# Decode attention with grouped queries: 8 MB loads through two buffers, a TensorE loop over the heads, and both projections moved out of it

## The chip, the cores and the metric

The kernel runs on one core of one Trainium2 chip. The core has five engines that run side by side, each in the order of its own instructions: TensorE (PE, with its weight loads listed as PEld), VectorE (DVE), ScalarE (ACT), GpSimd (POOL) and SyncE (SP). Data comes from HBM through 16 DMA engines, which take transfers from queues; here nearly all transfers are issued by SP, on one queue. The metric is the time on the device in microseconds, the median of several runs. Lower is better.

## The reference

One decode step of a transformer block, in float32, for one token `x` of 512 numbers:

```python
h  = x + A(layernorm(x))      # A: attention over a cache
h2 = h + B(layernorm(h))      # B: bilinear GLU

def A(x):                     # 32 query heads, 8 key/value heads, 65,536 cached positions, 128 wide
    q = x @ wq                                    # 512 -> 32 x 128
    scores = q . k / sqrt(128)                    # each group of 4 query heads shares one k and v
    o = softmax(scores) . v                       # over all 65,536 positions
    return o.reshape(4096) @ wo                   # 4096 -> 512

def B(x):
    return ((x @ w_gate) * (x @ w_up)) @ w_down   # 512 -> 1792 -> 512
```

K and V are 268 MB each, the five weight matrices together 28 MB. Every byte of them is used once.

## The kernel before, in words

K is laid out transposed in HBM. Each of the 8 heads (a key/value head with its four query heads) goes through K in eight tiles of 4 MB (128 partitions with 8,192 numbers each, 32 KB a row), then through V in eight tiles of 4 MB. All these tiles, and the large weights at the end, pass through one pool `stream` of four buffers (line 45), each loaded by one DMA from SP (`load`, line 107). A load waits until PE has finished with the buffer's last tile.

The order of the instructions on each engine, and the waits between engines, come from a tile framework: the code is written in sequence, the framework adds the semaphores, and every instruction of every head is its own (nothing loops on the chip).

A head runs like this. wq's share for this head (1 MB) is loaded into the pool `wts`; 16 small matmuls with the weights as the stationary side give the four query vectors as columns (line 139), and DVE puts them into a zero-padded `q_pad` (line 142). For a K tile, 16 matmuls with 512 columns write scores into one PSUM bank (line 154); the padding places each result in its own row, so that two tiles fill a bank of 128 rows. ACT copies a full bank to SBUF (line 160), DVE takes row maxima (line 161). After the last K tile the maxima are joined by a transpose on PE, a reduction, and a matmul that spreads them over the partitions (lines 165 to 177). ACT takes the exponential with row sums (line 184), PE transposes the probabilities (line 188), DVE copies them out (line 191). Then `pva` is zeroed by matmuls with a tile of zeros (line 218), and V's tiles are multiplied into it (line 232). DVE copies the rows out, four matmuls fold them to columns (line 242), and the result is divided by the sum. wo's share of this head (1 MB) is multiplied at once and added to `attn`, which gathers over the heads (line 249).

After the last head come the sum with x (folded into `attn` by matmuls on `x_oct`, line 212), the second layernorm, gate and up projection (line 285), the product, and the down projection into `pd` (line 323). wg is one load; wu comes in three pieces and wd in five, of falling size (lines 253 to 261). The output is stored at line 328.

Of the kernel before, what the change touches and what calls it, by code (L numbers as in the profile page):

```python
# [1 line left out]

# [6 lines left out]
F32 = mybir.dt.float32  # L18
AF = mybir.ActivationFunctionType
ALU = mybir.AluOpType  # L20
# [6 lines left out]
CK = 8192  # L27
# [5 lines left out]
NC = F // P  # L33
SCALE = DH ** -0.5
EPS = 1e-5


@with_exitstack
def body(ctx: ExitStack, tc: tile.TileContext, xc, xr, kT, v, wq, wo, wg, wu, wd, out):
    nc = tc.nc  # L40
    PS = bass.MemoryType.PSUM
    const = ctx.enter_context(tc.tile_pool(name="const", bufs=1))
    stream = ctx.enter_context(tc.tile_pool(name="stream", bufs=4))
    wts = ctx.enter_context(tc.tile_pool(name="wts", bufs=2))
    sbig = ctx.enter_context(tc.tile_pool(name="sbig", bufs=6))
    small = ctx.enter_context(tc.tile_pool(name="small", bufs=2))
    ps_sc = ctx.enter_context(tc.tile_pool(name="ps_sc", bufs=2, space=PS))
    ps_tp = ctx.enter_context(tc.tile_pool(name="ps_tp", bufs=2, space=PS))
    ps_va = ctx.enter_context(tc.tile_pool(name="ps_va", bufs=1, space=PS))
    ps_at = ctx.enter_context(tc.tile_pool(name="ps_at", bufs=1, space=PS))  # L50
    ps_sm = ctx.enter_context(tc.tile_pool(name="ps_sm", bufs=2, space=PS))

    def ctile(shape, name):
        return const.tile(shape, F32, tag=name, name=name)

    x_col = ctile([P, KT], "x_col")
    nc.scalar.dma_start(x_col, xc)
    ident = ctile([P, P], "ident")
    make_identity(nc, ident)
    mean_m = ctile([P, P], "mean_m")  # L60
    nc.vector.memset(mean_m, 1.0 / D)
    ones = ctile([P, P], "ones")
    nc.vector.memset(ones, 1.0)
    eps_t = ctile([P, 1], "eps_t")
    nc.vector.memset(eps_t, EPS)
    sel_h = ctile([P, REP], "sel_h")
    nc.vector.tensor_reduce(
        out=sel_h, in_=ident.rearrange("p (g h) -> p h g", h=REP), axis=AX.X, op=ALU.add)
    x_oct = ctile([8, D // 8], "x_oct")
    sel_b = ctile([P, 16], "sel_b")  # L70
    nc.vector.tensor_reduce(
        out=sel_b, in_=ident.rearrange("p (j c) -> p c j", j=4)[:, 0:16, :], axis=AX.X, op=ALU.add)
    sel_q = ctile([P, 4], "sel_q")
    nc.vector.tensor_copy(sel_q, ident.rearrange("p (j c) -> p c j", j=4)[:, 0, :])
    sel_1 = ctile([P, 1], "sel_1")
    nc.vector.tensor_reduce(out=sel_1, in_=sel_q, axis=AX.X, op=ALU.add)
    neg_mean = ctile([P, P], "neg_mean")
    nc.vector.tensor_scalar(
        out=neg_mean, in0=mean_m, scalar1=sel_1[:, 0:1], scalar2=-1.0, op0=ALU.mult, op1=ALU.mult)

    PADW = 2 * 28 + REP
    q_pad = [ctile([P, PADW], f"q_pad{i}") for i in range(2)]
    o_pad = [ctile([P, REP, 32], f"o_pad{i}") for i in range(2)]
    hn_pad = ctile([P, KT, 32], "hn_pad")
    f_pad = ctile([P, NC, 32], "f_pad")
    sel_pad = ctile([P, 32], "sel_pad")
    zeros = ctile([P, 512], "zeros")
    for t in (*q_pad, *o_pad, hn_pad, f_pad, sel_pad, zeros):
        nc.gpsimd.memset(t, 0.0)

    nc.vector.tensor_copy(sel_pad[:, 0:1], sel_1)

    def rstd_of(c, name):

        sq = small.tile([P, KT], F32, tag="ln_q", name=f"{name}_q")
        nc.vector.tensor_tensor(out=sq, in0=c, in1=c, op=ALU.mult)
        s2 = small.tile([P, 1], F32, tag="ln_s", name=f"{name}_s2")
        nc.vector.tensor_reduce(out=s2, in_=sq, axis=AX.X, op=ALU.add)
        pv = ps_sm.tile([P, 512], F32, tag="sm", name=f"{name}_pv")
        nc.tensor.matmul(pv[:, 0:1], mean_m, s2, start=True, stop=True)  # L100
        std = small.tile([P, 1], F32, tag="ln_t", name=f"{name}_t")
        nc.scalar.activation(std, pv[:, 0:1], AF.Sqrt, bias=eps_t[:, 0:1], scale=1.0)
        rstd = small.tile([P, 1], F32, tag="ln_r", name=f"{name}_r")
        nc.vector.reciprocal(rstd, std)
        return rstd

    def load(shape_cols, src, name, parts=P):
        t = stream.tile([P, CK], F32, tag="stream", name=name)
        nc.sync.dma_start(t[:parts, :shape_cols], src)  # L109
        return t  # L110

    wq_sb = wts.tile([P, KT, 512], F32, tag="wq", name="wq0")
    nc.sync.dma_start(wq_sb, wq[0])  # L113

    xn = ctile([P, KT], "xn")
    s1 = small.tile([P, 1], F32, tag="ln_s", name="ln1_s")
    nc.vector.tensor_reduce(out=s1, in_=x_col, axis=AX.X, op=ALU.add)
    pm = ps_sm.tile([P, 512], F32, tag="sm", name="ln1_pm")
    nc.tensor.matmul(pm[:, 0:1], mean_m, s1, start=True, stop=True)
    mean = small.tile([P, 1], F32, tag="ln_m", name="ln1_m")  # L120
    nc.vector.tensor_copy(mean, pm[:, 0:1])
    xd = small.tile([P, KT], F32, tag="ln_d", name="ln1_d")
    nc.vector.tensor_scalar(
        out=xd, in0=x_col, scalar1=mean[:, 0:1], scalar2=None, op0=ALU.subtract)
    rstd1 = rstd_of(xd, "ln1")
    nc.vector.tensor_scalar(  # L126
        out=xn, in0=xd, scalar1=rstd1[:, 0:1], scalar2=None, op0=ALU.mult)

    attn = ps_at.tile([P, 512], F32, tag="attn", name="attn")

    for h in range(HKV):
        if h > 0:
            wq_sb = wts.tile([P, KT, 512], F32, tag="wq", name=f"wq{h}")
            nc.sync.dma_start(wq_sb, wq[h])
        pq = ps_sm.tile([P, 512], F32, tag="sm", name=f"pq{h}")
        for r in range(REP):
            for k in range(KT):
                nc.tensor.matmul(  # L138
                    pq[:, r:r + 1], wq_sb[:, k, r * P:(r + 1) * P], xn[:, k:k + 1],
                    start=(k == 0), stop=(k == KT - 1))  # L140
        qp = q_pad[h % 2]
        nc.vector.tensor_copy(qp[:, 28:28 + REP], pq[:, 0:REP])

        scores = []
        mx = small.tile([P, 4], F32, tag="mx", name=f"mx{h}")
        for s in range(NT // 2):
            psc = ps_sc.tile([P, 512], F32, tag="sc", name=f"psc{h}_{s}")
            for half in range(2):
                n = 2 * s + half
                kt = load(CK, kT[h, n], f"k{h}_{n}")  # L150
                for r4 in range(4):
                    rs = 4 * half + r4
                    for j in range(4):
                        nc.tensor.matmul(  # L154
                            psc[32 * j:32 * j + 32, :],
                            qp[:, 28 - 4 * rs:60 - 4 * rs],
                            kt[:, (4 * r4 + j) * 512:(4 * r4 + j + 1) * 512],
                            start=(rs == 0), stop=(rs == 7))
            sc = sbig.tile([P, 512], F32, tag="scores", name=f"sc{h}_{s}")
            nc.scalar.copy(sc, psc)  # L160
            nc.vector.tensor_reduce(out=mx[:, s:s + 1], in_=sc, axis=AX.X, op=ALU.max)  # L161
            scores.append(sc)

        m1 = small.tile([P, 1], F32, tag="m1", name=f"m1_{h}")
        nc.vector.tensor_reduce(out=m1, in_=mx, axis=AX.X, op=ALU.max)  # L165
        pmx = ps_sm.tile([P, 512], F32, tag="sm", name=f"pmx{h}")
        nc.tensor.transpose(pmx[0:1, 0:P], m1, ident)  # L167
        mrow = small.tile([1, REP], F32, tag="mrow", name=f"mrow{h}")
        nc.vector.tensor_reduce(
            out=mrow, in_=pmx[0:1, 0:P].rearrange("p (g h) -> p h g", h=REP), axis=AX.X, op=ALU.max)  # L170
        mexp = small.tile([1, 32, REP], F32, tag="mexp", name=f"mexp{h}")
        nc.vector.tensor_copy(mexp, mrow.unsqueeze(1).to_broadcast([1, 32, REP]))  # L172
        pmb = ps_sm.tile([P, 512], F32, tag="sm", name=f"pmb{h}")
        nc.tensor.matmul(  # L174
            pmb[:, 0:1], mexp.rearrange("p g h -> p (g h)"), ones[0:1, 0:1], start=True, stop=True)
        nbias = small.tile([P, 1], F32, tag="nbias", name=f"nbias{h}")
        nc.vector.tensor_scalar(  # L177
            out=nbias, in0=pmb[:, 0:1], scalar1=-SCALE, scalar2=None, op0=ALU.mult)

        sums = small.tile([P, 4], F32, tag="sums", name=f"sums{h}")  # L180
        probs = []
        for s in range(NT // 2):
            sc = scores[s]
# [184 lines left out]
```

## Time and profile before

| | |
|---|---|
| median of 3 runs | 1320.65 us (1320.31 to 1320.68) |
| profiled execution: span from first to last instruction | 1319.2 us |
| median less that span | 1.45 us |
| PE busy, PE instructions (matmuls and weight loads) | 62%, 9,876 |
| DVE, ACT busy | 5%, 4% |
| DMA: bytes read, mean rate | 564.66 MB, 429 GB/s |
| granted TensorE clock, mean | 0.754 |
| instruction fetches by DMA | 38 packets, 0.62 MB |

The page divides the span into 40 slices. The chain of waits is followed back from the last instruction: each piece is either work or a transfer that was being waited for. The windows list, for a stretch of time, the busy time of each engine, the granted clock, the mean busy share of the 16 DMA engines and the bytes per second. Of the profiled execution the profile gives the span alone; what lies around it is taken as the 1.45 us between the span and the median.

### The profile page before, as it was taken

Reading aid. Unit: us, or ns where it says so; the run is one execution under the profiler, and the core shown is the slowest. Engines: PE = TensorE matmul, PEld = TensorE weight load, DVE = VectorE, ACT = ScalarE, POOL = GpSimd, SP = SyncE. Lnnn points to the kernel's source line nnn. Section 1 sums busy time; section 2 is a strip of 40 time slices with the busy share of each in tenths; the row PEclk is TensorE's granted clock in tenths of the full one; section 3 lists DMA queues with packets and bytes.
Section 4 is the critical chain, followed back from the end, with each engine's and each line's share of the span. In section 5 each row is a group of like instructions: output and inputs, shape, how many; then the busy total and the mean of one; then the engine's idle time right before and its main releaser. Section 6 shows DMA issues by size and latency. Waiting matters only on the chain.

```text
span 1319.2 us, 10572 instructions
## 1 busy us (share of the span) xinstructions
PE 818.6 (62%) x4938; PEld 244.9 (19%) x4938; DVE 66.8 (5%) x170; ACT 47.9 (4%) x104; POOL 2.2 (0%) x14
## 2 busy tenths in 40 slices
PE   5566476665757566665665666556575555665567
PEld 3111031211212112121211212112121121211114
DVE  1000000100001000010000100001000010000000
ACT  0010000100001000010000100001000000001000
POOL 0000000000000000000000000000000000000000
PEclk9867877767776787776877768777777777877767
DMA  9999999999999999999999999999999999999997
GB/s 401 434 436 429 430 435 432 435 433 431 430 437 430 433 431 434 434 432 430 434 435 430 432 434 431 437 430 432 432 435 433 430 432 430 438 431 431 431 430 314
DMA packets 22674, 565.33 MB, mean 429 GB/s; under 512 B 2660, under 2 KB 2664, under 8 KB 3304
## 3 DMA queue, kind: packets, MB, share of 16 engines
q1 hardware_dynamic: 22488, 564.67, 99.4%
q8 instruction: 38, 0.62, 0.2%
q10 hardware_dynamic: 144, 0.00, 0.0%
q14 instruction: 4, 0.03, 0.0%
HBM read 564.66 MB, written 0.00 MB: 428 GB/s over the span
## 4 chain that ended last, share of the span: by engine, by line
DMA 85%; PE 14%; issue 0%; SPq 0%; DVE 0%
DMA k<-in_kT 42%; DMA v<-in_v 41%; PE psc L154 7%; PE pva L232 7%; DMA wd<-in_wd 2%; PE pd L323 0%; SPq L109 0%; SPq L113 0%; DVE y L327 0%
## 5 line engine op out<-in xcount | busy, mean ns | idle before, releaser
L154 PE MATMUL psc<-k,q_pad 128*32 128x512 f32 x2048 | 345.7, 837 | 227.4 <-DMA k<-in_kT 227.4
L232 PE MATMUL pva<-v,pt 128*16 128x512 f32 x2048 | 338.3, 821 | 216.9 <-DMA v<-in_v 216.9
L154 PEld LDWEIGHTS psc<-k,q_pad 128*32 128x32 f32 x2048 | 83.6, 147 | 492.7 <-issue 293.9
L232 PEld LDWEIGHTS pva<-v,pt 128*16 128x16 f32 x2048 | 66.4, 122 | 481.6 <-DMA v<-in_v 271.2
L160 ACT COPY sc<-psc 128x512 f32<-128x512 f32 x32 | 18.8, 586 | 1147.7 <-PE psc L154 1147.7
L161 DVE TENSOR_REDUCE mx<-sc 128x1 f32<-128x512 f32 x32 | 22.0, 686 | 584.3 <-ACT sc L160 584.3
L138 PE MATMUL pq<-xn,wq 128*128 128x1 f32 x256 | 39.3, 288 | 0.8 <-DVE xn L126 0.8
L138 PEld LDWEIGHTS pq<-xn,wq 128*128 128x128 f32 x256 | 38.8, 243 | 0.9 <-DVE xn L126 0.9
L188 PE MATMUL ptp<-ident,sc 128*128 128x128 f32 x128 | 30.5, 413 | 10.9 <-ACT sc L184 10.5
L239 DVE COPY orow<-pva 128x512 f32<-128x512 f32 x8 | 5.5, 692 | 553.4 <-PE pva L232 553.4
L218 PE MATMUL pva<-zeros 128*32 128x512 f32 x64 | 26.7, 1025 | 0.0
L249 PE MATMUL attn<-wo,o_pad 128*32 128x512 f32 x64 | 26.5, 1049 | 0.3 <-DVE o_pad L246 0.3
L188 PEld LDWEIGHTS ptp<-ident,sc 128*128 128x128 f32 x128 | 23.0, 212 | 15.9 <-ACT sc L184 12.2
L184 ACT ACTIVATE sc<-sc,nbias 128x512 f32<-128x512 f32 x32 | 22.7, 711 | 18.5 <-DVE nbias L177 18.5
L191 DVE COPY pt<-ptp 128x512 f32<-128x512 f32 x32 | 22.1, 692 | 23.0 <-PE ptp L188 22.3
L242 PE MATMUL po<-sel_b,orow 128*128 128x4 f32 x64 | 8.5, 256 | 6.5 <-DVE orow L239 6.5
L242 PEld LDWEIGHTS po<-sel_b,orow 128*128 128x128 f32 x64 | 7.8, 191 | 13.9 <-DVE orow L239 13.9
L167 PE MATMUL pmx<-ident,m 128*1 128x128 f32 x8 | 2.2, 270 | 12.4 <-DVE m L165 12.4
L202 PE MATMUL pl<-l,ones 128*128 128x4 f32 x16 | 4.3, 339 | 7.4 <-DVE l L199 7.4
L174 PE MATMUL pmb<-ones,mexp 1*128 1x1 f32 x16 | 3.8, 306 | 5.0 <-DVE mexp L172 5.0
L323 PE MATMUL pd<-wd,f_pad 128*32 128x128 f32 x112 | 6.1, 417 | 1.2 <-DMA wd<-in_wd 1.2
L323 PEld LDWEIGHTS pd<-wd,f_pad 128*32 128x32 f32 x112 | 5.8, 174 | 1.2 <-DVE f_pad L318 1.2
(76 smaller groups left out, 72.8 us busy)
## 6 DMA issues: line engine op xcount, KB each, us to landing
k<-in_kT SPq DMA_DIRECT2D x64, 4096.0 KB, 34.3
v<-in_v SPq DMA_DIRECT2D x63, 4096.0 KB, 35.0
wq<-in_wq SPq DMA_DIRECT2D x8, 1024.0 KB, 34.8
wo<-in_wo SPq DMA_DIRECT2D x8, 1024.0 KB, 35.4
v<-in_v SPq DMA_DIRECT2D x4, 1024.0 KB, 30.3
wg<-in_wg SPq DMA_DIRECT2D x1, 3584.0 KB, 31.7
wu<-in_wu SPq DMA_DIRECT2D x1, 1792.0 KB
wu<-in_wu SPq DMA_DIRECT2D x2, 896.0 KB, 27.3
```

The source lines that it names most:

```text
L138: nc.tensor.matmul(pq[:, r:r + 1], wq_sb[:, k, r * P:(r + 1) * P], xn[:, k:k + 1], start=(k == 0), stop=(k == KT - 1))
L154: nc.tensor.matmul(psc[32 * j:32 * j + 32, :], qp[:, 28 - 4 * rs:60 - 4 * rs], kt[:, (4 * r4 + j) * 512:(4 * r4 + j + 1) * 512], start=(rs ...
L160: nc.scalar.copy(sc, psc)
L161: nc.vector.tensor_reduce(out=mx[:, s:s + 1], in_=sc, axis=AX.X, op=ALU.max)
L184: nc.scalar.activation(sc, sc, AF.Exp, bias=nbias[:, 0:1], scale=SCALE, accum_out=sums[:, s:s + 1])
L188: nc.tensor.transpose(ptp[:, b * P:(b + 1) * P], sc[:, b * P:(b + 1) * P], ident)
L191: nc.vector.tensor_copy(pt.rearrange("p g b h -> p b g h"), ptp.rearrange("p (b g h) -> p b g h", b=4, h=REP))
L218: nc.tensor.matmul(pva[32 * j:32 * j + 32, :], zeros[:, 0:32], zeros, start=True, stop=False)
L232: nc.tensor.matmul(pva[32 * j:32 * j + 16, :], pt[:, 8 * j + rs, :, :].rearrange("p b h -> p (b h)"), vt[:, (4 * r4 + j) * 512:(4 * r4 + j ...
L242: nc.tensor.matmul(po[:, 0:REP], orow[:, b * P:(b + 1) * P], sel_b[:, 4 * b:4 * b + 4], start=(b == 0), stop=(b == 3))
L249: nc.tensor.matmul(attn[32 * r:32 * r + 32, :], op[:, r, :], wo_sb[:, r, :], start=(h == 0), stop=(h == HKV - 1))
L323: nc.tensor.matmul(pd[32 * j:32 * j + 32, 0:P], f_pad[:, c, :], wd_t[:, o:o + P], start=False, stop=(c == NC - 1))
```

## The change

The kernel is written without the framework: SBUF places, semaphores and waits are given by hand.

- K and V come in tiles of 8 MB (16,384 numbers, 64 KB a row), four of each per head, through two buffers `slots`. SP issues all loads in order; a load waits for a count of PE (`c_pe`) that says that its buffer has been read.
- PE's instructions for a head are written once, in a loop on the chip over the 8 heads (`PE.Fori`). Inside it PE waits on semaphores that it counts down again itself (`take`), since the same instruction must wait anew in each pass. The other engines' instructions are still written out for each head.
- wq is one load of 8 MB, first of all. All 32 query vectors are computed before the first head, with the normalised x as the stationary side and wq streaming (32 wide matmuls into two banks), then turned into columns by 8 small matmuls with `sel_q`. Each head copies its own from `q_all` to `q_pad`.
- An 8 MB K tile fills a bank by itself; the four banks of a head stay in PSUM. Maxima and exponentials read PSUM; the copy by ACT is gone. `pva` is cleared once at the start; the first V matmuls of a head start afresh on the rows that they write.
- The heads' results are kept in `o_pad` (all 32), and wo is loaded once behind the last V, in two pieces of 6 and 2 MB, and applied in one go.
- x is added at the end through PE from `xd` and `x_pad`; `x_oct` and its load are gone. wg, wu and wd come after wo; wd has its own place, in cuts of 4, 4, 3, 2 and 1 chunks.

```diff
-CK = 8192
+CK = 16384
+WO_CUT = 6 * REP * D
+WU_CUTS = (0, 2, 3, 4)
+WD_CUTS = (0, 4, 8, 11, 13, 14)
...
+    slots = [sb("slot_a", P, CK, offset=SLOT_A), sb("slot_b", P, CK, offset=SLOT_B)]
+    wd_t = sb("wd_t", P, NC * D, offset=SLOT_C)
...
+    SP.dma_start(slots[0], wq).then_inc(slot_sem[0], 16)
+    SP.dma_start(slots[1], kT[0, 0]).then_inc(slot_sem[1], 16)
...
+            src = kT[h, n] if n < NT else v[h, n - NT]
+            m = h * 2 * NT + n - 2
...
+            SP.dma_start(slots[i % 2], src)._wait_ge(c_pe.sem, free).then_inc(slot_sem[i % 2], 16)
...
+    SP.wait_ge(c_pe.sem, pe_at(HKV - 1, V_DONE + NT - 2))
+    for lo, hi in ((0, WO_CUT), (WO_CUT, CK)):
+        wo_sems.append(next(tail))
+        SP.dma_start(wo_t[:, lo:hi], wo[:, lo:hi]).then_inc(wo_sems[-1], 16)
+    SP.wait_ge(c_pe.sem, pe_at(HKV - 1, V_DONE + NT - 1))
...
+    def take(sem, n=1):
+        PE.sem_inc(sem, -n).wait_op(sem, n, "sem-ge")
...
+    for i in range(2):
+        for k in range(KT):
+            for j in range(4):
+                o = k * HKV * 512 + (4 * i + j) * 512
+                ins = PE.matmul(
+                    psc[i][32 * j:32 * j + 32, :], xn_pad[:, k, :], slots[0][:, o:o + 512],
+                    start=(k == 0), stop=(k == KT - 1))
...
+    with PE.Fori(0, HKV):
+        take(dve_pe)
+        for n in range(NT):
+            s = (n + 1) % 2
+            take(slot_sem[s], 16)
+            for rs in range(8):
+                for j in range(4):
+                    o = (4 * rs + j) * 512
+                    ins = PE.matmul(
+                        psc[n][32 * j:32 * j + 32, :], q_pad[:, 28 - 4 * rs:60 - 4 * rs],
+                        slots[s][:, o:o + 512], start=(rs == 0), stop=(rs == 7))
+            pe(ins)
...
+        for n in range(NT):
+            take(act_pe)
+            if n >= 2:
+                take(dve_pe)
+            for b in range(4):
+                ins = PE.transpose(ptp[n % 2][:, b * P:(b + 1) * P], sc[n][:, b * P:(b + 1) * P], ident)
+            pe(ins)
+        for n in range(NT):
+            s = (n + 1) % 2
+            take(slot_sem[s], 16)
+            if n >= 2:
+                take(dve_pe)
...
+    for kk in range(HKV * REP):
+        if kk * D in (0, WO_CUT):
+            PE.wait_ge(wo_sems[kk > 0], 16)
```

More of the change, by code (lines that the diff above doesn't have):

```diff
@@ L10 @@
-from contextlib import ExitStack
 import concourse.bass as bass
-import concourse.tile as tile
 from concourse import mybir
-from concourse._compat import with_exitstack
-from concourse.masks import make_identity
 F32 = mybir.dt.float32
@@ L33 @@
 NC = F // P
+NB = CK // 512
 SCALE = DH ** -0.5
 EPS = 1e-5
[L38 to L129, printed above, removed]
[L131 to L281 removed]
@@ L292, in body @@
-    g_sb = ctile([P, FJ], "g_sb")
-    nc.scalar.activation(g_sb, pg[:, :FJ], AF.Copy, scale=rstd2[:, 0:1])
-    project(pu, wu_t)
-    pd = ps_va.tile([P, 512], F32, tag="va", name="pd")
-    for j in range(4):
-        nc.tensor.matmul(
-            pd[32 * j:32 * j + 32, 0:P], sel_pad, arow[:, j * P:(j + 1) * P],
-            start=True, stop=False)
-    f_sb = ctile([P, FJ], "f_sb")
-    for half in range(2):
-        cs = slice(half * 256, min(FJ, half * 256 + 256))
-        nc.vector.scalar_tensor_tensor(
-            out=f_sb[:, cs], in0=pu[:, cs], scalar=rstd2[:, 0:1], in1=g_sb[:, cs],
-            op0=ALU.mult, op1=ALU.mult)
@@ L306, in body @@
-    pfs = [ps_sm.tile([P, 512], F32, tag="sm", name=f"pf{i}") for i in range(2)]
-    for b in range(3):
-        nc.tensor.matmul(
-            pfs[b // 2][:, 4 * (b % 2):4 * (b % 2) + 4], f_sb[:, b * P:(b + 1) * P], sel_q,
-            start=(b != 1), stop=(b == 1))
-        if b == 1:
-            nc.vector.tensor_copy(f_pad[:, 0:8, 0], pfs[0][:, 0:8])
-    for i in range(2):
-        nc.tensor.matmul(
-            pfs[1][64 * i:64 * i + 64, 4:6], f_sb[:, 3 * P:FJ], sel_q[:, 2 * i:2 * i + 2],
-            start=False, stop=True)
@@ L318, in body @@
-    nc.vector.tensor_copy(f_pad[:, 8:NC, 0], pfs[1][:, 0:6])
+    assert pe(ins) == Q_ROWS
+    PE.wait_ge(c_dve.sem, q_rows)
+    for i in range(2):
+        for r in range(REP):
+            ins = PE.matmul(
+                ptp[i][:, 4 * r:4 * r + 4], q_row[i][:, r * P:(r + 1) * P], sel_q,
+                start=True, stop=True)
+        t = pe(ins)
+    assert t == Q_COLS == BASE
+    with PE.Fori(0, HKV):
[6 more added lines that the diff above has]
+                    o = (4 * rs + j) * 512
+                    ins = PE.matmul(
+                        psc[n][32 * j:32 * j + 32, :], q_pad[:, 28 - 4 * rs:60 - 4 * rs],
+                        slots[s][:, o:o + 512], start=(rs == 0), stop=(rs == 7))
+            pe(ins)
+        take(dve_pe)
+        pe(PE.transpose(psm[0:1, 0:P], m1, ident))
+        take(dve_pe)
+        pe(PE.matmul(
+            psm[:, 128:129], m_exp.rearrange("p g h -> p (g h)"), ones[0:1, 0:1],
+            start=True, stop=True))
+        for n in range(NT):
+            take(act_pe)
+            if n >= 2:
+                take(dve_pe)
+            for b in range(4):
+                ins = PE.transpose(ptp[n % 2][:, b * P:(b + 1) * P], sc[n][:, b * P:(b + 1) * P], ident)
+            pe(ins)
+        for n in range(NT):
+            s = (n + 1) % 2
+            take(slot_sem[s], 16)
+            if n >= 2:
+                take(dve_pe)
+            for rs in range(8):
+                for j in range(4):
+                    o = (4 * rs + j) * 512
+                    ins = PE.matmul(
+                        pva[32 * j:32 * j + 16, :],
+                        pt[n][:, 8 * j + rs, :, :].rearrange("p b h -> p (b h)"),
+                        slots[s][:, o:o + 512],
+                        start=(n == 0 and rs == 0), stop=(n == NT - 1 and rs == 7))
+            pe(ins)
+        take(dve_pe)
+        pe(PE.matmul(psm[:, 132:132 + REP], ones, l4, start=True, stop=True))
+        take(dve_pe)
+        for b in range(4):
+            ins = PE.matmul(
+                ptp[1][:, 0:REP], o_row[:, b * P:(b + 1) * P], sel_b[:, 4 * b:4 * b + 4],
+                start=(b == 0), stop=(b == 3))
+        pe(ins)
@@ new lines, in body @@
+    assert c_pe.n == BASE + PER_HEAD
+    c_pe.n = BASE + HKV * PER_HEAD
+    attn, pg, pu, pac, pv, pd = psc[0], psc[1], psc[2], psm, psc[3], pva
+    PE.wait_ge(c_dve.sem, o_done)
+    for kk in range(HKV * REP):
+        if kk * D in (0, WO_CUT):
+            PE.wait_ge(wo_sems[kk > 0], 16)
+        j = kk % 4
+        ins = PE.matmul(
+            attn[32 * j:32 * j + 32, :], o_pad[:, kk, :], wo_t[:, kk * D:(kk + 1) * D],
+            start=(kk < 4), stop=(kk >= HKV * REP - 4))
+    attn_done = pe(ins)
@@ new lines, in body @@
+    rsum, s2b, std2, rstd2 = (stat[:, k:k + 1] for k in range(8, 12))
+    a_done = c_act.up(ACT.activation(
+        a_row, attn, AF.Copy, accum_out=rsum)._wait_ge(c_pe.sem, attn_done))
+    nm_done = dve(DVE.tensor_scalar(
+        out=nmean, in0=neg_mean, scalar1=rsum, scalar2=None, op0=ALU.mult)._wait_ge(
+            c_act.sem, a_done))
+    PE.matmul(pac[:, 0:KT], ident, xd, start=True, stop=False)
+    for j in range(4):
+        PE.matmul(pd[32 * j:32 * j + 32, 0:P], x_pad[:, j, :], ident, start=True, stop=False)
@@ new lines, in body @@
+    PE.wait_ge(c_act.sem, a_done)
+    for k in range(KT):
+        PE.matmul(
+            pac[:, k:k + 1], a_row[:, k * P:(k + 1) * P], sel_1, start=False, stop=False)
+    hc_done = pe(PE.matmul(
+        pac[:, 0:KT], nmean, ones[:, 0:KT], start=False, stop=True)._wait_ge(c_dve.sem, nm_done))
+    for j in range(4):
+        PE.matmul(
+            pd[32 * j:32 * j + 32, 0:P], sel_pad, a_row[:, j * P:(j + 1) * P],
+            start=False, stop=False)
+    hn_done = t = dve(DVE.tensor_copy(hn_pad[:, :, 0], pac[:, 0:KT])._wait_ge(c_pe.sem, hc_done))
@@ new lines, in body @@
+    t = dve(DVE.tensor_tensor(
+        out=hq, in0=hn_pad[:, :, 0], in1=hn_pad[:, :, 0], op=ALU.mult)._wait_ge(c_dve.sem, t))
+    hq_done = dve(DVE.tensor_reduce(out=s2b, in_=hq, axis=AX.X, op=ALU.add)._wait_ge(c_dve.sem, t))
+    var_done = pe(PE.matmul(pv[:, 0:1], mean_m, s2b, start=True, stop=True)._wait_ge(
+        c_dve.sem, hq_done))
+    std_done = c_act.up(ACT.activation(
+        std2, pv[:, 0:1], AF.Sqrt, bias=eps_t[:, 0:1], scale=1.0)._wait_ge(c_pe.sem, var_done))
+    rstd_done = dve(DVE.reciprocal(rstd2, std2)._wait_ge(c_act.sem, std_done))
@@ new lines, in project @@
+    def project(acc, w0, sems):
+        for k in range(KT):
+            if k in sems:
+                PE.wait_ge(sems[k], 16)
+            for j in range(4):
+                o = (w0 + k) * F + j * FJ
+                ins = PE.matmul(
+                    acc[32 * j:32 * j + 32, :FJ], hn_pad[:, k, :], wgu_t[:, o:o + FJ],
+                    start=(k == 0), stop=(k == KT - 1))
+        return pe(ins)
+    pg_done = project(pg, 0, {0: wg_sem})
+    ACT.wait_ge(c_dve.sem, rstd_done)
+    g_done = c_act.up(ACT.activation(
+        g_sb, pg[:, :FJ], AF.Copy, scale=rstd2)._wait_ge(c_pe.sem, pg_done))
@@ new lines, in body @@
+    pu_done = project(pu, KT, dict(wu_sems))
+    DVE.wait_ge(c_act.sem, g_done)
+    DVE.wait_ge(c_pe.sem, pu_done)
+    f_done = []
+    for lo, hi in ((0, 256), (256, FJ)):
+        f_done.append(dve(DVE.scalar_tensor_tensor(
+            out=f_sb[:, lo:hi], in0=pu[:, lo:hi], scalar=rstd2, in1=g_sb[:, lo:hi],
+            op0=ALU.mult, op1=ALU.mult)))
+    pf = [t[:, 0:16] for t in ptp]
+    PE.wait_ge(c_dve.sem, f_done[0])
+    for b in range(2):
+        ins = PE.matmul(
+            pf[0][:, 4 * b:4 * b + 4], f_sb[:, b * P:(b + 1) * P], sel_q, start=True, stop=True)
@@ new lines, in body @@
+    pf0_done = pe(ins)
+    PE.wait_ge(c_dve.sem, f_done[1])
+    PE.matmul(pf[1][:, 0:4], f_sb[:, 2 * P:3 * P], sel_q, start=True, stop=True)
+    for i in range(2):
+        ins = PE.matmul(
+            pf[1][64 * i:64 * i + 64, 4:6], f_sb[:, 3 * P:FJ], sel_q[:, 2 * i:2 * i + 2],
+            start=False, stop=True, skip_group_check=True)
+    pf1_done = pe(ins)
+    fp0_done = dve(DVE.tensor_copy(f_pad[:, 0:8, 0], pf[0][:, 0:8])._wait_ge(c_pe.sem, pf0_done))
+    fp1_done = dve(DVE.tensor_copy(f_pad[:, 8:NC, 0], pf[1][:, 0:6])._wait_ge(c_pe.sem, pf1_done))
@@ L320, in body @@
+    PE.wait_ge(c_dve.sem, fp0_done)
+    wd_at = dict(wd_sems)
     for c in range(NC):
+        if c in wd_at:
+            PE.wait_ge(wd_at[c], 16)
+        if c == 8:
+            PE.wait_ge(c_dve.sem, fp1_done)
         for j in range(4):
             o = c * D + j * P
-            nc.tensor.matmul(
+            ins = PE.matmul(
                 pd[32 * j:32 * j + 32, 0:P], f_pad[:, c, :], wd_t[:, o:o + P],
                 start=False, stop=(c == NC - 1))
-    y = ctile([P, P], "y")
-    nc.vector.tensor_copy(y, pd[:, 0:P])
@@ L328, in body @@
-    nc.sync.dma_start(out, y.rearrange("(j r) n -> j r n", j=4)[:, 0, :])
+    pd_done = pe(ins)
+    y_done = dve(DVE.tensor_copy(y, pd[:, 0:P])._wait_ge(c_pe.sem, pd_done))
+    SP.dma_start(out, y[0:P:32, :])._wait_ge(
+        c_dve.sem, y_done).then_inc(sem_out, 16)
+    SP.wait_ge(sem_out, 16)
 def kernel(A_x, A_k_cache, A_v_cache, A_wq, A_wo, B_x, B_w_gate, B_w_up, B_w_down):
@@ L363 @@
     out = nc.dram_tensor("out_y", (4, P), F32, kind="ExternalOutput").ap()
-    with tile.TileContext(nc) as tc:
-        body(tc, *args, out)
+    body(nc, *args, out)
     r = run_bass_kernel_spmd(nc, [{f"in_{n}": a for n, a in arrays.items()}], core_ids=[0])
```

270 lines of the change are left out of this document (176 added, 94 removed).

## The prediction

> **What bounds the kernel now.** I read the page first, then the chain of waits, then short windows at the end.
>
> ```profile
> span 1319.2 us, 10572 instructions
> ...
> PE 818.6 (62%) x4938; PEld 244.9 (19%) x4938; DVE 66.8 (5%) x170; ACT 47.9 (4%) x104; POOL 2.2 (0%) x14
> ...
> DMA  9999999999999999999999999999999999999997
> ...
> DMA packets 22674, 565.33 MB, mean 429 GB/s; under 512 B 2660, under 2 KB 2664, under 8 KB 3304
> ...
> q1 hardware_dynamic: 22488, 564.67, 99.4%
> q8 instruction: 38, 0.62, 0.2%
> ...
> DMA 85%; PE 14%; issue 0%; SPq 0%; DVE 0%
> ```
>
> The DMA engines are busy 99.4% of the span with the kernel's own data, in every slice but the last. The 14% of PE on the chain is not a second bound: it is PE freeing a buffer so that a load can be issued, while three other loads are still in flight. So a change of compute is worth nothing here. What counts is the bytes, what each packet costs beyond its bytes, whether the queue ever runs dry, and the two ends.
>
> The bytes hardly change: all of K, V and the weights is still read once. The end is more telling. The windows (us, busy time of PE, PEld, DVE, ACT, POOL with counts, clock, DMA share, GB/s) and then the chain's last pieces:
>
> ```profile
> 500.00:700.00 200.00, 123.11 (x745) 33.70 (x741) 9.09 (x20) 6.45 (x14) 0.00 (x0) 0.76 1.00 433
> ...
> 1306.00:1308.00 2.00, 1.31 (x13) 0.20 (x9) 0.58 (x2) 0.00 (x0) 0.00 (x0) 1.00 0.81 327
> 1308.00:1310.00 2.00, 1.00 (x10) 0.90 (x10) 0.57 (x3) 0.00 (x0) 0.00 (x0) 0.79 0.49 203
> 1310.00:1312.00 2.00, 1.84 (x36) 1.88 (x40) 0.00 (x0) 0.00 (x0) 0.00 (x0) 0.50 0.48 202
> 1312.00:1314.00 2.00, 2.00 (x45) 2.00 (x41) 0.00 (x0) 0.00 (x0) 0.00 (x0) 0.50 0.46 182
> 1314.00:1316.00 2.00, 2.00 (x46) 1.90 (x36) 0.00 (x0) 0.00 (x0) 0.00 (x0) 0.50 0.07 26
> ```
>
> ```profile
> 1285.98 24.04 DMA wd<-in_wd
> ...
> 1310.15 6.13 PE pd L323 x112
> ...
> 1316.30 0.29 DVE y L327
> ```
>
> The DMA share does not fade out; it steps from 1.00 to one half and stays there (0.49, 0.48, 0.46) until about 1314.3. So eight of the sixteen engines finish near 1307.2 and the other eight some 7.1 us later, though each was given the same eight rows of every load. Something took 7.1 us from one half. The only traffic on the page that isn't shared equally by rows is q8, the instruction fetches: 0.2% of 16 x 1319.2 us is 42 us of engine time (32 to 53, by rounding), which on eight engines is 4 to 7 us each. I read the late half as the engines that fetch instructions. That is inference: the page does not name an engine. With 38 fetches on eight engines, 4.75 each, one fetch then costs its engine 7.1 / 4.75 = 1.5 us.
>
> **The change part by part.** The compute it drops or moves, with what the idle PE would give for it:
>
> ```profile
> L154 PE MATMUL psc<-k,q_pad 128*32 128x512 f32 x2048 | 345.7, 837 | 227.4 <-DMA k<-in_kT 227.4
> L232 PE MATMUL pva<-v,pt 128*16 128x512 f32 x2048 | 338.3, 821 | 216.9 <-DMA v<-in_v 216.9
> ...
> L160 ACT COPY sc<-psc 128x512 f32<-128x512 f32 x32 | 18.8, 586 | 1147.7 <-PE psc L154 1147.7
> ...
> L138 PE MATMUL pq<-xn,wq 128*128 128x1 f32 x256 | 39.3, 288 | 0.8 <-DVE xn L126 0.8
> ...
> L188 PE MATMUL ptp<-ident,sc 128*128 128x128 f32 x128 | 30.5, 413 | 10.9 <-ACT sc L184 10.5
> ...
> L218 PE MATMUL pva<-zeros 128*32 128x512 f32 x64 | 26.7, 1025 | 0.0
> ```
>
> Gone are 39.3 us of query matmuls (replaced by 32 wide ones), 26.7 us of zeroing pva, and 18.8 us of score copies on ACT (maxima and exponentials now read PSUM). PE sat idle 227.4 + 216.9 us waiting for K and V, so all of this lay under DMA: 0 us, and if the cover were gone it would be a gain, not a loss.
>
> *Do two buffers keep the queue full?* Here the change could lose, so I work it at the slowest rows of PE's timeline:
>
> ```profile
> 517.52 5.19 PE L154 MATMUL psc<-k,q_pad 128*32 128x512 f32 x32 [6.12 <-DMA k<-in_kT]
> ...
> 565.86 6.61 PE L154 MATMUL psc<-k,q_pad 128*32 128x512 f32 x32 [3.32 <-DMA k<-in_kT]
> ...
> 581.94 5.39 PE L232 MATMUL pva<-v,pt 128*16 128x512 f32 x32
> 587.62 3.63 PE L232 MATMUL pva<-v,pt 128*16 128x512 f32 x32 [0.29 <-DMA v<-in_v]
> ...
> 646.75 5.32 PE L232 MATMUL pva<-v,pt 128*16 128x512 f32 x32 [4.55 <-DMA v<-in_v]
> 652.88 1.05 PE L242 MATMUL po<-sel_b,orow 128*128 128x4 f32 x8 [0.81 <-DVE orow L239]
> ```
>
> Six tiles start 517.52 to 565.86, so a 4 MB load takes 9.67 us and an 8 MB one 19.3. PE needs 3.63 to 6.61 us per tile, 7.3 to 13.2 per 8 MB. A load is issued when its buffer is released, while the other buffer's load is running: 13.2 against 19.3 leaves 6.1. The softmax sits between the last K and the first V: 565.86 + 6.61 = 572.5 to 581.94 is 9.5 us, so the first V starts at 13.2 + 9.5 = 22.7 after the last K landed and releases its buffer at 35.9, against 2 x 19.3 = 38.7 when the queue would be empty: 2.8 us to spare at the slowest clock, 7 at 5.5 us per tile. At the head's end, from 652.07 to 653.93 PE works 1.9 us for o; then comes the jump back, and the next K must start by 38.7 - 13.2 = 25.5, so the jump may take 10 us. All SP loads stand in one queue, each behind a wait for PE; nothing else is on that queue until wo, wg, wu, wd, which wait for the last two V buffers and are issued 6 us early in the same way. At the start wq (8 MB) lands near 22 and its matmuls end by 35, before K0 lands at 41. So 0 us; bounds 0 to the price in the second rival.
>
> *Larger packets.* Each load has 128 rows, eight per engine, whatever the row's length. Before: (22674 - 2660) / 16 = 1251 data packets per engine and 166 small ones. After: 64 + 1 + 2 + 1 + 3 + 5 = 76 loads, 608 data packets and about 76 completions, so some 730 fewer. A packet's fixed price: in the 1312 to 1314 window, mostly 2 KB rows, 182 / 0.46 = 396 GB/s at full share, against 433 with 32 KB rows, so 2 KB takes 82.8 instead of 75.7 ns, 7 ns more. Shares above 1 elsewhere say that packets overlap a little, so I take 5 ns: **-3.6 us**. Bounds: -5.1 (7 ns) and -1.1, if a 64 KB row, larger than any packet in this trace, is cut in two.
>
> *The loop.* PE runs 9,876 instructions with 38 fetches of 0.62 MB / 38 = 16.3 KB: one fetch for 260 instructions. One head is (4096 + 4096) / 8 = 1024 for K and V, 32 for transposes and some 26 small ones, 1,082: 4.2 fetches, 68 KB. Unrolled, every one is new; in the loop the same 68 KB run eight times. If they stay, PE fetches its code once: about 1,082 + 700 around it, 7 fetches, at most one or two per engine: the late half costs 1.5 instead of 7.1, **-5.6 us**. If nothing stays, it is 4.2 fetches a pass and one more for each jump, 8 x 5.2 + 3 = 45, 5.6 per engine, 8.4 us: +1.3. The trace of before repeats no instruction and can't decide. [...]
>
> [...]
>
> *The end.* wd's first cut shrinks from six chunks to four, and the last is one chunk either way. Before, all 112 pd matmuls began at 1310.15, after wd's first piece (1310.02), and ended 2.0 us after the last data (1316.28 against 1314.3). Starting earlier, they can end about 1.2 us after it: **-0.8**, bounds 0 and -1.5. y and its store are unchanged. Attention's projection moves behind the last head, but under 25 us of wg, wu and wd still loading (11 MB at 433 GB/s): 0.
>
> Sum: 1319.2 - 3.6 - 5.6 - 0.8 = 1309.2 us of span. The median run is 1320.65, 1.45 above the span, so **1310.7**.
>
> **Rivals.**
> (1) *The loop fetches as much as before*, or the late half has another cause. For it: one fetch per 260 instructions in the only trace there is. Then 1320.65 - 3.6 - 0.8 + 1.3 = 1317.6; 1316 with no extra fetch per jump, 1320 with cut rows as well, 1323 if a jump refetches the whole body on top (8 x 8.4 + 3 = 70 fetches, 13 us on the late half).
> (2) *The two buffers run dry at the softmax* (slower). Place: the first V of each head, from the point where it starts later than 38.7 - 13.2 = 25.5 us after the last K landed. Against it are the 2.8 us above; for it, PE's code in that stretch may come late, from engines that now hold 64 KB packets, each 2.4 us at 433 / 16 = 27 GB/s. Two such waits, 4.8 us, overrun by 2 us, eight times 16 us; by 4 us, 32. With the gains of (1) at -3.1, from 1333.6 to 1349.6; 1334.
> (3) *Longer rows read more slowly.* At 2% less than 433 GB/s the loads cost 26 us: 1337. For it only that no 64 KB row is in the trace; against it, 2 KB to 32 KB rows differ by their packets' fixed price alone. [...]
>
> **How the numbers follow.** Forecast 0.48, rival (1) 0.36, (2) 0.10, (3) 0.06. The measurement can tell 0.2%, 2.6 us: faster is below 1318.0, slower above 1323.3. All of the forecast and a third of (1) are faster: 0.60. Two thirds less a little of (1), 0.21, are the same; (2), (3) and the top of (1) are slower: 0.19. The range goes from 1308 (7 ns a packet, -1.5 at the end) over nearly all of (1): 1308 to 1322. The forecast's own is 1308 to 1314.
>
> **What would show it.** q8's count: about 8 if the code stays, 38 or more if not. The DMA share at the end: no step at one half, if the late half was the fetches. Data packets: near 10,000, or 18,000 if rows are cut. The share in the middle at 1.00 and 434 GB/s, and no DMA gap at the head's middle. The prediction is wrong if PE's waits before the first V or after the jump bring the queue to a stop, or if the late half stays with few fetches.

## The result, and the profile after

The changed kernel takes **1310.63 us** (four runs, 1310.47 to 1310.67) against 1320.48 us before on the same chip: a ratio of 0.9927, 95% interval 0.9913 to 0.9941. The forecast was 1310.7.

The page of the changed kernel, the lines that answer to those of before:

```profile
span 1309.3 us, 9941 instructions
...
PE 669.7 (51%) x4692; PEld 201.7 (15%) x4692; DVE 69.2 (5%) x177; ACT 28.0 (2%) x72; POOL 2.6 (0%) x13
...
DMA packets 11107, 564.81 MB, mean 431 GB/s; under 512 B 1364, under 2 KB 1368, under 8 KB 2008
...
q1 hardware_dynamic: 10952, 564.67, 99.6%
q8 instruction: 7, 0.11, 0.0%
```

PE is busy 149 us less (818.6 to 669.7), and none of that is in the time: the DMA engines still carry the same 564.67 MB at 99.6%. Two counts have moved. The data packets are (11107 - 1364) / 16 = 609 per engine in place of 1251, so a row of 64 KB goes as one packet (the trace has 8,320 of 65,536 bytes, one for each row of wq, K and V). And q8 shows 7 instruction fetches where there were 38, though PE executes nearly as many instructions, 2 x 4,692. In the trace none of the 7 starts between 186.4 and 1288.4 us, a stretch that holds the loop's passes 2 to 8.

The windows at the end, with the same columns as before:

```profile
500.00:700.00 200.00, 94.63 (x669) 27.28 (x669) 9.03 (x20) 2.79 (x8) 0.00 (x0) 0.73 1.00 435
...
1300.00:1302.00 2.00, 0.84 (x32) 0.57 (x24) 0.00 (x0) 0.00 (x0) 0.00 (x0) 0.96 0.98 409
1302.00:1304.00 2.00, 2.00 (x40) 1.45 (x39) 0.00 (x0) 0.00 (x0) 0.00 (x0) 0.50 0.91 365
1304.00:1306.00 2.00, 2.00 (x48) 1.41 (x40) 0.00 (x0) 0.00 (x0) 0.00 (x0) 0.68 0.20 79
1306.00:1308.00 2.00, 0.02 (x3) 0.00 (x0) 0.29 (x1) 0.00 (x0) 0.00 (x0) 1.00 0.01 5
```

The seven microseconds at a share of one half are gone; the share falls from 0.98 to 0.20 within two windows. The sixteen landings of the last piece of wd now lie within 1.8 us; before, they were 7.7 us apart. In the middle the rate is 435 GB/s, so rows of 64 KB are read no more slowly. The last matmuls, from the chain of waits:

```profile
1301.85 4.21 PE pva L407 x80
...
1306.08 0.29 DVE y L411
```

They end at 1306.06. Where the data end shows in windows of 1 us:

```profile
1304.00:1305.00 1.00, 1.00 (x24) 0.77 (x17) 0.00 (x0) 0.00 (x0) 0.00 (x0) 0.50 0.38 148
1305.00:1306.00 1.00, 1.00 (x32) 0.64 (x24) 0.00 (x0) 0.00 (x0) 0.00 (x0) 0.87 0.03 10
```

Bytes still come after 1305. In the trace the last packet of a row of wd ends at 1305.28, and the last piece is seen to have landed at 1305.55; PE begins the last chunk at 1305.59. So PE ends 0.8 us after the last packet. Before, it was 1.7 us: the last packet ended at 1314.59, PE at 1316.28.

PE's timeline over one softmax and one jump back of the loop:

```profile
571.71 1.90 PE L276 MATMUL psc<-slot_a,q_pad 128*32 128x512 f32 x16
...
577.19 3.44 PE L291 MATMUL ptp<-ident,sc 128*128 128x128 f32 x16 [1.15 <-PEq L244]
584.53 8.98 PE L301 MATMUL pva<-slot_b,pt 128*16 128x512 f32 x64 [3.90 <-PEq L244]
603.85 9.57 PE L301 MATMUL pva<-slot_a,pt 128*16 128x512 f32 x64 [10.33 <-PEq L244]
...
642.60 8.96 PE L301 MATMUL pva<-slot_a,pt 128*16 128x512 f32 x64 [10.93 <-PEq L244]
...
652.47 1.03 PE L311 MATMUL ptp<-sel_b,o_row 128*128 128x4 f32 x8 [0.59 <-PEq L244]
661.82 9.61 PE L276 MATMUL psc<-slot_b,q_pad 128*32 128x512 f32 x64 [8.33 <-PEq L244]
```

The waits inside the loop are counted to PE's own sequencer (`take`, L244), so the releaser's name says little; the spacing says more. Each 8 MB buffer is begun 19.2 to 19.3 us after the one before (584.53, 603.85; 642.60, 661.82), which is the load alone, also across the softmax and across the jump. PE was ready 3.9 us before the first V landed, and released its buffer at 593.5, 10.3 us before it began on the next load.

### The profile page after: what moved, and what is told of

Read it like the earlier page. It is cut to its first block, busy times and chain, and to the rows that moved or that the text cites. A ratio compares the mean times of both kernels' runs of the same rounds, so it can differ in the third digit from the quotient of the medians.

```text
span 1309.3 us, 9941 instructions
## 1 busy us (share of the span) xinstructions
PE 669.7 (51%) x4692; PEld 201.7 (15%) x4692; DVE 69.2 (5%) x177; ACT 28.0 (2%) x72; POOL 2.6 (0%) x13
## 2 busy tenths in 40 slices
DMA packets 11107, 564.81 MB, mean 431 GB/s; under 512 B 1364, under 2 KB 1368, under 8 KB 2008
## 3 DMA queue, kind: packets, MB, share of 16 engines
q1 hardware_dynamic: 10952, 564.67, 99.6%
## 5 line engine op out<-in xcount | busy, mean ns | idle before, releaser
L276 PE MATMUL psc<-slot_a,q_pad 128*32 128x512 f32 x1024 | 147.6, 741 | 164.5 <-PEq L244 164.5
L301 PE MATMUL pva<-slot_a,pt 128*16 128x512 f32 x1024 | 146.2, 735 | 162.0 <-PEq L244 162.0
L276 PE MATMUL psc<-slot_b,q_pad 128*32 128x512 f32 x1024 | 145.7, 733 | 143.0 <-PEq L244 143.0
L301 PE MATMUL pva<-slot_b,pt 128*16 128x512 f32 x1024 | 147.1, 739 | 105.4 <-PEq L244 105.4
L276 PEld LDWEIGHTS psc<-slot_a,q_pad 128*32 128x32 f32 x1024 | 40.7, 133 | 271.4 <-issue 271.4
L276 PEld LDWEIGHTS psc<-slot_b,q_pad 128*32 128x32 f32 x1024 | 40.2, 132 | 242.0 <-issue 242.0
L301 PEld LDWEIGHTS pva<-slot_a,pt 128*16 128x16 f32 x1024 | 34.4, 112 | 273.7 <-issue 273.7
L301 PEld LDWEIGHTS pva<-slot_b,pt 128*16 128x16 f32 x1024 | 34.7, 113 | 213.7 <-issue 213.7
L203 DVE TENSOR_REDUCE mx<-psc 128x1 f32<-128x512 f32 x32 | 22.1, 692 | 582.9 <-PE psc L276 582.9
L216 ACT ACTIVATE sc<-psc,nbias 128x512 f32<-128x512 f32 x32 | 21.6, 686 | 1159.5 <-DVE nbias L212 1159.5
```

The costliest lines, as they stand in the source:

```text
L203: t = dve(DVE.tensor_reduce(out=mx[:, n:n + 1], in_=psc[n], axis=AX.X, op=ALU.max)._wait_ge(c_pe.sem, pe_at(h, K_DONE + n)))
L216: e = ACT.activation(sc[n], psc[n], AF.Exp, bias=nbias[:, 0:1], scale=SCALE, accum_out=sums[:, n:n + 1])
L276: ins = PE.matmul(psc[n][32 * j:32 * j + 32, :], q_pad[:, 28 - 4 * rs:60 - 4 * rs], slots[s][:, o:o + 512], start=(rs == 0), stop=(rs == 7))
L301: ins = PE.matmul(pva[32 * j:32 * j + 16, :], pt[n][:, 8 * j + rs, :, :].rearrange("p b h -> p (b h)"), slots[s][:, o:o + 512], start=(n = ...
```

## The experiments

Each is the changed kernel with one edit, unless said otherwise. Differences are between medians on the same chip.

### The base

The changed kernel itself, beside two of the three groups.

> The changed kernel itself, on the chip of the runs beside it: 1310.6 us again, 7 instruction fetches, no step at one half at the end. It is the base for the three kernels beside it.

Measured: 1310.97 us (1310.27 to 1311.27), ratio 0.9929 (0.9915 to 0.9942) to the kernel before at 1320.13.

> The changed kernel again, beside the two kernels with other cuts of wd: 1310.6 to 1311.0 us, PE ending 1.7 us after the last data.

Measured: 1310.76 us (1310.51 to 1311.41), ratio 0.9926 (0.9912 to 0.9939). Medians of one kernel differ by 0.3 us between chips; smaller differences are not read. Measured by the last packet, PE ends 0.8 us after the data in the first of these two profiles (1306.25 against 1305.49) and 1.2 us after it in the second (1306.67 against 1305.43), not 1.7.

### PE's heads written out

```diff
-    with PE.Fori(0, HKV):
+    for h in range(HKV):
```

> The changed kernel with PE's eight heads written out instead of looped; nothing else differs. My reading (the late half of the DMA engines before were those that fetched instructions, and the loop's code stays in PE's store): about 9,384 / 260 = 36 fetches, the DMA share again stands at one half for some 6 to 7 us at the end, and the time rises by 29 more fetches / 8 engines x 1.5 us = 5.4 us, to 1316.0. Rival (the late half came from something else that the change removed, such as four buffers, the many small loads or rows of 32 KB): fetches rise to 36, but no step at one half, and 1310.6 within 1 us.

Measured: 1316.87 us (1316.18 to 1317.17), ratio 0.9974 (0.9964 to 0.9984) to before, **+5.9** on the base. The instruction queue of its page, and its windows at the end:

```profile
q8 instruction: 37, 0.61, 0.2%
```

```profile
1302.00:1304.00 2.00, 0.96 (x8) 0.16 (x8) 0.28 (x1) 0.00 (x0) 0.00 (x0) 1.00 1.01 419
1304.00:1306.00 2.00, 1.75 (x38) 1.71 (x42) 0.86 (x4) 0.00 (x0) 0.00 (x0) 1.00 0.66 272
1306.00:1308.00 2.00, 0.84 (x24) 0.53 (x20) 0.00 (x0) 0.00 (x0) 0.00 (x0) 0.80 0.49 203
1308.00:1310.00 2.00, 2.00 (x43) 1.48 (x39) 0.00 (x0) 0.00 (x0) 0.00 (x0) 0.50 0.45 175
1310.00:1312.00 2.00, 1.62 (x40) 0.91 (x32) 0.29 (x1) 0.00 (x0) 0.00 (x0) 0.85 0.09 32
```

With the fetches the step at one half comes back (0.49, 0.45), in a kernel that keeps two buffers, 64 KB packets and the few weight loads. So the late half goes with the fetches, and the rival cause falls. 30 more fetches on eight engines are 3.75 each: 5.9 / 3.75 = 1.57 us of its engine's time for one fetch of 16 KB.

The landings in the traces show it fetch by fetch. Each load leaves sixteen landings, as many as there are DMA engines. In the changed kernel the landings of the load that is complete at 42.0 us lie within 0.6 us. After the first fetch (46.1 us) one of the sixteen is late, by 1.7 us, while the others stay within 0.6; after two fetches two are late, and after five (load complete at 198.1 us) five, by 1.5 to 1.9 us. With the heads written out it goes on: after seven fetches and one of the other instruction queue, q14, eight are late, by 1.4 to 2.3 us, and after 33 it is still eight, by 5.9 to 7.2 us, while the other eight stay within 1.3. As I read these counts (one late after one fetch, five after five, never more than eight), each fetch holds up one engine of a fixed half, and the delay stays with it to the end.

### Two heads in the loop's body

```diff
-    with PE.Fori(0, HKV):
+    with PE.Fori(0, HKV // 2):
+        for _ in range(2):
+            take(dve_pe)
...
```

> [...] If PE's store keeps any loop body, 11 or 12 fetches and 1311 us. [...]

Measured: 1317.99 us (1317.57 to 1318.75), ratio 0.9983 (0.9974 to 0.9993) to before: **+7.1** on the kernel with 32 idle matmuls on the same chip (1310.87), which itself stands at its base. Its instruction queue, and PE behind the first jump back:

```profile
q8 instruction: 44, 0.72, 0.2%
```

```profile
343.77 1.03 PE L312 MATMUL ptp<-sel_b,o_row 128*128 128x4 f32 x8 [0.59 <-PEq L244]
353.80 2.74 PE L277 MATMUL psc<-slot_b,q_pad 128*32 128x512 f32 x9 [9.00 <-PEq L244]
359.05 7.72 PE L277 MATMUL psc<-slot_b,q_pad 128*32 128x512 f32 x55 [2.51 <-issue]
```

Four passes of two heads do the same work with twice the code in the body: 2 x 1,082 = 2,164 matmuls and weight loads, which at one fetch of 16.3 KB for 260 (38 fetches before) I estimate at 136 KB in place of 68. A loop alone does not save fetches: with this body there are 44, 7 more than written out, so I read it as fetched again in every pass. The same price fits: 37 / 8 x 1.5 = 7 us. Here PE also stops for 2.5 us after nine matmuls of the new pass; a fetch starts at 356.7 us, right behind the stop, so I read it as a wait for code. That stall is covered by the load that is running: the DMA share is 0.98 from 350 to 355 us and 0.95 from 355 to 360.

### Rows of K and V in two and in eight pieces

In HBM the pieces of a tile lie one behind the other, each with 128 short rows; the same with 8 in place of 2.

```diff
-            SP.dma_start(slots[i % 2], src)._wait_ge(c_pe.sem, free).then_inc(slot_sem[i % 2], 16)
+            SP.dma_start(
+                slots[i % 2].rearrange("p (c n) -> p c n", c=2),
+                src.rearrange("c p n -> p c n"))._wait_ge(c_pe.sem, free).then_inc(slot_sem[i % 2], 16)
...
-        "v": lay(A_v_cache, HKV, NT, P, TPC * DH),
+        "v": lay(A_v_cache, HKV, NT, P, 2, CK // 2, perm=(0, 1, 3, 2, 4)),
```

> The changed kernel with each 64 KB row of K and V stored and loaded as two pieces of 32 KB that don't adjoin in HBM; each load stays 8 MB and one instruction. 64 x 8 = 512 more data packets per engine. At 5 ns a packet +2.6 us, 1313.2; at 7 ns +3.6. Rival (packets overlap, their fixed price is hidden): no change, 1310.6.

Measured: 1313.12 us (1312.79 to 1313.35), ratio 0.9946 (0.9932 to 0.9959) to before, **+2.15** on the base.

> As the kernel with two pieces, but eight pieces of 8 KB: 64 x 8 x 7 = 3,584 more data packets per engine. At 5 ns a packet +17.9 us, 1328.5; at 7 ns +25 us, 1335.7. Rival (price hidden): 1310.6. It measures the price of a packet by itself.

Measured: 1327.42 us (1327.23 to 1327.92), **+16.45**; slower than the kernel before, ratio 1.0055 (1.0042 to 1.0069). The packet counts of the two pages:

```profile
DMA packets 19299, 564.81 MB, mean 431 GB/s; under 512 B 1364, under 2 KB 1368, under 8 KB 2008
```

```profile
DMA packets 68451, 564.81 MB, mean 426 GB/s; under 512 B 1364, under 2 KB 1368, under 8 KB 2008
```

(19299 - 11107) / 16 = 512 and (68451 - 11107) / 16 = 3,584 packets more per engine: 2150 / 512 = 4.2 ns and 16450 / 3584 = 4.6 ns a packet. The price is nearly the same for each packet and it is not hidden; the 5 ns taken were near, the 7 ns of the window too much. In both kernels the pieces of a row also lie apart in HBM, which was not tested by itself.

### More work for PE before the first V

The matmuls write a bank that is free at that place; for 64 of them the count is 16 in place of 8.

```diff
+        for rs in range(8):
+            for j in range(4):
+                PE.matmul(psc[3][32 * j:32 * j + 32, :], q_pad[:, 28:60], sc[3], start=True, stop=True)
         for n in range(NT):
```

> The changed kernel with 32 idle matmuls (128x512, their result unused) before the first V of each head: 9 us of PE work at the mean rate, 13 at the slowest. In the changed kernel PE stood ready 3.9 us before the first V landed, and that buffer was released 10.3 us before the next load had landed: 14 us of room. My reading (two buffers suffice with room to spare): no change within 1 us; at the slowest clock the queue may run dry by up to 3 us in a head, +25 at most. Rival (two buffers are at their limit): each us added comes out, 8 x 9 = +72 us.

Measured: 1310.87 us (1310.79 to 1311.13): **no change**. The added matmuls of the same head:

```profile
581.25 8.12 PE L295 MATMUL psc<-sc,q_pad 128*32 128x512 f32 x64
```

> The same with 64 idle matmuls, 18 us at the mean rate: more than the 14 us of room, so the queue runs dry 4 us a head: about +33 us, 1344 (between +15 and +100 with PE's clock). The DMA share then shows gaps. If there is still no change, something else than the release of the buffer sets the time of the next load.

Measured: 1331.26 us (1329.36 to 1332.24), ratio 1.0083 (1.0067 to 1.0098) to before, **+20.4** on the kernel with 32. Its instruction queue, its timeline and two of its windows:

```profile
q8 instruction: 8, 0.13, 0.0%
```

```profile
587.97 14.68 PE L295 MATMUL psc<-sc,q_pad 128*32 128x512 f32 x128
602.48 7.04 PE L306 MATMUL pva<-slot_b,pt 128*16 128x512 f32 x64
609.85 7.06 PE L306 MATMUL pva<-slot_a,pt 128*16 128x512 f32 x64 [0.32 <-PEq L244]
631.74 9.80 PE L306 MATMUL pva<-slot_b,pt 128*16 128x512 f32 x64 [14.83 <-PEq L244]
```

```profile
600.00:605.00 5.00, 5.00 (x52) 1.26 (x48) 0.00 (x0) 0.00 (x0) 0.00 (x0) 1.00 0.97 419
605.00:610.00 5.00, 4.68 (x48) 1.12 (x44) 0.00 (x0) 0.00 (x0) 0.00 (x0) 1.00 0.49 210
```

The second rival's mechanism is real, and it decides where it was expected, only the kernel is far from it. With 14.7 us of added work the first V's buffer is released at 609.5, and the load into it is begun by PE at 631.74, 21.9 us after the one before (609.85) in place of 19.3: 2.6 us lost, and 20.4 over the eight heads are 2.55 for each. The share of 0.49 in the window from 605 shows the missing packets, but it is no measure of the loss: in these views a packet counts whole in the window in which it starts (from 606 to 607 us the share is 2.42, in the next two windows 0.00). Between the 8.1 us that cost nothing and these 14.7 lies the point: 14.7 - 2.55 is about 12 us of room for a head. That is less than the 14.2 expected. The buffer was free 0.3 us before PE began on the next load, and time was lost all the same; as I read it, a new load had to be issued some 2 us (an estimate: 14.2 less 12) before the running one was seen to have landed. The expected +33 came out as +20.4, since the 64 matmuls took 14.7 us and not 18, and the room is 12 us and not 14.

### Other cuts of wd

```diff
-WD_CUTS = (0, 4, 8, 11, 13, 14)
+WD_CUTS = (0, 6, 10, 12, 13, 14)
```

```diff
-WD_CUTS = (0, 4, 8, 11, 13, 14)
+WD_CUTS = (0, 4, 6, 8, 10, 11, 12, 13, 14)
```

> The changed kernel with the old cuts of wd, 6, 4, 2, 1 and 1 chunks in place of 4, 4, 3, 2, 1. My prediction gave the smaller first cut 0.8 us: 1311.6. Rival: in the changed kernel PE waits for the second piece anyway (80 of 112 matmuls begin at 1301.85, behind its landing), and the second old piece ends with chunk 10 instead of 8, so the end depends on the clock of the last 4 us alone: within 0.5 us of the base.

> The changed kernel with wd in eight pieces of 4, 2, 2, 2, 1, 1, 1 and 1 chunks: PE can go on after the first 4 chunks 1.2 us earlier. If PE's last 80 matmuls set the end, they end up to 0.8 us nearer to the last data: 1310.0; 24 more small packets per engine cost 0.1 us. Rival: the last landing sets the end: no change.

Measured: 1310.75 us (1310.61 to 1311.17) with the old cuts and 1310.86 (1310.34 to 1310.93) with the finer, beside 1310.76: **no change** either way. The pd matmuls in the base of that chip, and with the finer cuts, there with two windows:

```profile
1299.78 1.08 PE L407 MATMUL pva<-wd_t,f_pad 128*32 128x128 f32 x32
1302.02 1.08 PE L407 MATMUL pva<-wd_t,f_pad 128*32 128x128 f32 x32 [1.16 <-DMA wd_t<-in_wd]
1303.92 2.75 PE L407 MATMUL pva<-wd_t,f_pad 128*32 128x128 f32 x48 [0.82 <-DMA wd_t<-in_wd]
```

```profile
1300.41 6.12 PE L407 MATMUL pva<-wd_t,f_pad 128*32 128x128 f32 x112
```

```profile
1302.00:1304.00 2.00, 2.00 (x44) 1.82 (x40) 0.00 (x0) 0.00 (x0) 0.00 (x0) 0.50 1.07 413
1304.00:1306.00 2.00, 2.00 (x44) 1.43 (x36) 0.00 (x0) 0.00 (x0) 0.00 (x0) 0.50 0.40 153
```

With finer cuts the 112 run almost without a pause, but they take 6.12 us, 55 ns each, at a granted clock of 0.50 from 1302 to 1306, where the base of this chip needs 34 ns in its first two groups. And the last group still waits: in the trace the last piece is seen to land at 1306.06 and its matmuls begin at 1306.11. So PE ended at 1306.5, not clearly earlier than the base at 1306.7, and the rival holds here: the last landing sets the end. The same is seen with the old cuts (1305.66 and 1305.75) and in the first profile of the changed kernel (1305.55 and 1305.59); only in the base of this chip does PE come 0.3 us behind (1305.72 and 1306.02).

### Three parts undone together

The heads written out, the rows in two pieces, and the old cuts of wd.

> Three parts undone together: heads written out, K and V rows in two pieces of 32 KB, wd in the old cuts; the two buffers of 8 MB, the queries first and wo at the end stay. If the parts add up, 1311.0 + 5.9 + 2.2 + up to 0.8 = 1319.1 to 1319.9, that is the kernel before within 1 us, and buffers and order are worth nothing. Rival (the order or the buffers carry part of the gain): 1317 or less.

Measured: 1318.84 us (1318.51 to 1319.43) against 1320.01 for the kernel before on that chip, ratio 0.9991 (0.9982 to 1.0000). The single prices add up: 1310.97 + 5.9 + 2.15 + 0 = 1319.0. Of the whole gain of 9.2 us, 1.2 is left for all else: wq and wo in rows of 64 KB (about 104 packets fewer per engine, 0.5 us at 4.4 ns), half the completions, one small load less, the order, the buffers, and the end, where PE finishes 0.8 us after the last packet in this kernel too (1313.96 against 1313.18), 1.7 us in the kernel before. These were not taken apart.

## Why the prediction was right

**What bounds it.** Right. 149 us less of PE work and 19.9 less of ACT bought nothing, and 8 us more of PE work a head cost nothing; the time moved with packets and fetches, and with PE's work only past its room of about 12 us a head.

**The late half.** Right, and now shown. The prediction read it off a step of the DMA share and one small queue, without a row that names an engine; writing the loop out brought the step back with the fetches, and the landings show one engine falling behind at each fetch. The price of 1.5 us a fetch measured 1.57. The packets of the 38 fetches themselves take 36 us in the trace, 4.5 us for each of eight engines; where the rest of the 7.1 comes from is not shown.

**The loop.** -5.6 predicted, 5.9 measured. Here the prediction chose between two ends without a row to decide it, and chose well: seven jumps back, 7 fetches in the whole run. That the code of the loop stays was the author's assumption, which no run had shown; the runs now show that it does, but not why. The one fetch more for each jump, in the sum of the other end, does not appear in this kernel: no fetch starts in passes 2 to 8. What the runs show besides is a size, by an estimate from the 16.3 KB for 260 instructions: bodies of 68 KB (7 fetches) and of some 84 KB (8, with the 64 idle matmuls, which are 128 matmuls in the trace, and as many weight loads) stay, one of about 136 KB does not (44).

**The packets.** The count was right (608 predicted, 609 measured), the row was not cut, and the price was a little high: 4.2 to 4.6 ns in place of 5. K's and V's rows give 2.15 us of the 3.6; with the 1.2 us that the three parts leave over, the term is at most 3.3. It was oversized by 0.3 us or more. Its reason for going below 7 ns was not sound: a share above 1 needs no overlap of packets, since a packet counts whole in the window in which it starts (the 2.42 with 64 idle matmuls above).

**The end.** This is the step that failed: the cut buys nothing, though the end became shorter by about as much as forecast. The smaller first cut was to be worth 0.8 us and is worth nothing (1310.75 us with the old cuts, 1310.76 with the new). PE does end nearer to the data, 0.8 us after the last packet in place of 1.7, but with the old cuts as well (1306.14 against 1305.38). The prediction's own 2.0 was counted from 1314.3, a mean over engines; the last packet ended at 1314.59. What the runs show in place of the cut is whether PE keeps up. Before, all 112 matmuls ran at a granted clock of 0.50, and the last chunk began 0.8 us after its piece was seen to land (1315.67 against 1314.91). In the changed kernel, with old, new or finer cuts, it begins within 0.1 us of that landing in four profiles and 0.3 us behind it in one. With the finer cuts the earlier start does this, at a clock of 0.50 throughout; with the old cuts a better clock does it (the first 48 matmuls in 1.84 us, 38 ns each). Why PE had that clock there and not before is not shown.

**The sum.** That the span of 1309.2 came out within 0.1 of the measured 1309.3 is partly luck. The three terms make 10.0 us; this chip gave 9.85, the chips of the two bases 9.2 and 9.5. Of the 9.2, the loop is 5.9, K's and V's rows are 2.15, the cut is 0, and 1.2 was not taken apart.

**Two buffers.** Right in sign, too cautious in size: 2.8 to 7 us of room were worked out, the trace shows 14.2 (3.9 before the landing, 10.3 behind it), and the added matmuls put it at about 12. PE took 8.3 to 9.9 us for 8 MB, not 13.2, which was the slowest tile twice (why one long run is faster than two short ones was not tested); and the softmax took 7.0 us (573.6 to 580.6) in place of 9.5.

**The rivals.** The first falls with 7 fetches; the second's mechanism exists at 15 us of added work and not below 8; the third falls with 435 GB/s in the middle. The 1323 under the first is 1322 by its own terms (1320.65 - 3.6 - 0.8 + 6.1).

## What to carry to other kernels

In a kernel that keeps all DMA engines busy, look at how the DMA share ends: if it stands at a fraction for some microseconds, some engines may have carried something that the others did not, and the small queues of the page are the place to look. Instructions were such a load here, so a loop on the engine with most of the instructions (PE, 9,876 of 10,572 before) paid here (5.9 us) where compute had no say at all, but only while its body was not fetched again in each pass: by the estimates above, 84 KB was not and 136 KB was. Long rows pay next, here by 4.2 to 4.6 ns for each packet saved.

## What was not expected of the hardware

- One fetch of 16 KB costs its DMA engine about 1.57 us of data time (the 5.9 / 3.75 above), as long as some 42 KB of K or V take at 435 / 16 = 27 GB/s, more than twice its own bytes. The packet itself is recorded with mostly 0.9 us (0.88 to 0.97 in the kernel before).
- The loop with too large a body fetches more (44) than the same code written out (37): 7 more over its three jumps back.
- PE's granted clock in the last microseconds differs between runs of one kernel: after the same pause, it was 0.50 from 1302 to 1304 in the first profile (80 matmuls in 4.21 us) and 1.00 in the base of the last chip (32 in 1.08 us). So a pause alone does not decide it, and what does is not shown.
